# Small TensorE products side by side, packed values in 32-column tiles, one PSUM pool and positions as 512 and 64

## The chip, the cores and the metric

One core of a Trainium2 chip runs the whole kernel. The metric is device time in microseconds (us), the median of several runs. The runs of the two kernels are made on the same chip in the same session. A run more than 1.5% above the fastest run of its kernel is called slow here, and ratios use fast runs alone. TensorE is called PE in the profile, its weight loads PEld; DVE is VectorE, ACT is ScalarE, POOL is GpSimd, SP issues DMA.

## The reference, cut to what matters

```python
# attention: batch 8, heads 8, 576 positions, 64 per head, 32 packed queries
p_packed = sm_attn(p, k, v)                  # 32 rows per head
out = sm_attn(q, p_packed, p_packed)         # 576 rows per head
# gate: x is out as [8, 576, 512]
proj = x @ w_proj                            # x1, x2, x3, 512 columns each
x2_conv = irfft(rfft(x2) * rfft(filter_fft)) # along the 576 positions
y = x1 * x2_conv * x3
return y @ w_out
```

The kernel never forms x. It projects the 32 packed rows of each head (qm), carries the second attention's weights through the Fourier transform, multiplies in the spectrum (f, tt, gm), and comes back with the inverse (x2).

Of the kernel before, what the change touches and what calls it, by code (L numbers as in the profile page):

```python
# [17 lines left out]
P = 128  # L18
# [8 lines left out]

# [4 lines left out]
COL0 = [320, 0, 448, 128, 256]  # L32
HALF = 288
# [4 lines left out]


def _column_t():  # L40
    t = np.zeros(576, dtype=np.int64)
    for i in range(5):
        t[COL0[i]:COL0[i] + TILE_SZ[i]] = TILE_T[i]
    return t


def _constants(S):
# [35 lines left out]
    ac = _f16(inv[:, :, _column_t()].transpose(1, 0, 2))  # L83
# [3 lines left out]
class Op:  # L87


    def __init__(self, n, engine, call, what, args, kw):  # L90
        self.n, self.engine, self.call, self.what, self.args, self.kw = n, engine, call, what, args, kw
        named = dict(kw)
        rest = [a for a in args if isinstance(a, bass.AP)]
        self.out = named.pop("out") if "out" in named else rest.pop(0)
        self.ins = rest + [a for a in named.values() if isinstance(a, bass.AP)]
        self.writes = [r for r in map(region, [self.out]) if r]
        self.reads = [r for r in map(region, self.ins) if r]
        self.columns = max([x.size() // x.shape[0] for x in [self.out] + self.ins[:1]])
        self.need, self.then = 0, []

    def small_tiles(self):
        return self.what == "matmul" and self.ins[0].shape[0] == 64
# [35 lines left out]
class Recorder:  # L138
# [5 lines left out]
    def __init__(self, tc):  # L144
        self.tc, self.ops, self.slot = tc, [], {}
        for name, engine in self.NAMES.items():
            setattr(self, name, self.Engine(self, engine, getattr(tc.nc, name)))

    class Engine:
# [3 lines left out]
        def __getattr__(self, what):  # L153
            def record(*args, **kw):
                ops = self.recorder.ops
                ops.append(Op(len(ops), self.engine, getattr(self.real, what), what, args, kw))
            return record

    def tile(self, pool, shape, dtype, tag, bufs, name):
        t = pool.tile(shape, dtype, tag=tag, name=name, bufs=bufs)  # L160
        self.slot[t.tensor.name] = tag, bufs
        return t

    def depend(self):

        seen, self.users, bank = {}, {}, {}
        for op in self.ops:
            before = set()
            for mine, regions in ((False, op.reads), (True, op.writes)):
                for t, p0, p1, cols in regions:  # L170
                    for o, theirs, q0, q1, c in seen.get(t, ()):
                        if (mine or theirs) and p0 < q1 and q0 < p1 and not cols.isdisjoint(c):
                            before.add(o)
# [13 lines left out]
    def plan(self):  # L187
# [3 lines left out]
        used = dict.fromkeys([tag for tag, _ in self.slot.values()], 0)  # L191
# [4 lines left out]
        window, busy, full, tiling = 3413.0, {}, {0: False}, [False]  # L196
# [16 lines left out]
        def clock(t):  # L213

            for k in range(max(full) + 1, int(t // window) + 1):
                full[k] = busy.get(k - 1, 0) > (0.22 if full[k - 1] else 0.72) * window
            return full[int(t // window)]

        def news(op):
            return {r[0] for r in op.writes + op.reads if r[0] in self.slot and r[0] not in opened}  # L220

        def fits(op):
            more = {}
            for t in news(op):
                tag, bufs = self.slot[t]
                more[tag] = more.get(tag, 0) + 1
                if used[tag] + more[tag] > bufs:
                    return False
# [9 lines left out]
        def issue(e, t):  # L238
            while free[e] <= t + 1e-6:
                op = min((o for o in ready[e] if fits(o)), key=lambda o: o.n, default=None)  # L240
                if op is None:
                    return
                ready[e].remove(op)
                for x in news(op):
                    used[self.slot[x][0]] += 1
                    opened.add(x)
                order.append(op)
                if op.what == "dma_start":
# [3 lines left out]
                    at(t + took + 1500, "start", op)  # L252
                else:
                    if e == "PE":
                        n, fast = op.columns, clock(t)
                        if op.small_tiles():
                            took = 40 if fast else 75
                        else:
                            took = max(n / 2.4 + 2.5, 26) if fast else max(n / 1.2, 45)
                        if op.small_tiles() != tiling[0]:  # L260
                            took += 95
                        tiling[0] = op.small_tiles()
                        k = int(t // window)
                        busy[k] = busy.get(k, 0) + took
                        land = took + (n / 2.4 if op.small_tiles() else 0) + 175
                    else:
                        took = op.ns()
                        land = took + 60
# [5 lines left out]
        for op in self.ops:  # L274
            if op.need == 0:
# [3 lines left out]
        while events:  # L279
            t, _, what, x = heapq.heappop(events)  # L280
            if what == "done":
                release(x, False)
                for r in {r[0] for r in x.reads + x.writes}:
                    if r in left:
                        left[r] -= 1
                        used[self.slot[r][0]] -= left[r] == 0
# [31 lines left out]
def kernel(  # L318
# [31 lines left out]
    ps = ctx.enter_context(tc.tile_pool(name="ps", bufs=3, space=bass.MemoryType.PSUM))  # L350
# [4 lines left out]
    NA = 3  # L355

    def pst(name, shape, dtype=FP32):
        return nc.tile(ps, shape, dtype, "pa", NA, name)

    def psm(name, shape, dtype=FP32):  # L360
        return nc.tile(ps, shape, dtype, "pm", 8 - NA, name)
# [109 lines left out]
    def front(b):  # L471
# [86 lines left out]
        pv = pst(f"pv_b{b}", [P, 2, 4 * D])  # L558
        z1 = pst(f"z1_b{b}", [P, 2])
        for t in range(2):  # L560
            for i in range(KI):
                nc.tensor.matmul(pv[:, t, :], e1[:, i, ts(t, P)], vn[:, 4 * t:4 * t + 4, ts(i, D)],
                                 start=(i == 0), stop=(i == KI - 1))
            for i in range(KI):
                nc.tensor.matmul(z1[:, t:t + 1], e1[:, i, ts(t, P)], ones[0:KP, :],
                                 start=(i == 0), stop=(i == KI - 1))
            if t == 0:
                yield 810
        rz1 = sb([P, 2], FP32, tag="rz1", name=f"rz1_b{b}")
        nc.vector.reciprocal(rz1[:], z1[:])  # L570
        ppn = sb([P, 2, D], FP16, tag="ppn", name=f"ppn_b{b}")
        for u in range(4):
            r = slice(32 * u, 32 * u + 32)
            nc.vector.tensor_tensor(out=ppn[r, :, :], in0=pv[r, :, ts(u, D)],
                                    in1=rz1[r, :].unsqueeze(2).broadcast_to([32, 2, D]), op=ALU.mult)
        yield 810
# [11 lines left out]
        e2 = sb([P, 4, HJ], FP16, tag="e2", name=f"e2_b{b}")  # L588
        e2c = sb([P, P], FP16, tag="e2c", name=f"e2c_b{b}")
        a2n = sb([P, 4, HJ], FP16, tag="a2n", name=f"a2n_b{b}")  # L590
        a2c = sb([P, P], FP16, tag="a2c", name=f"a2c_b{b}")
        zs = sb([P, 5, H], FP32, tag="zs", name=f"zs_b{b}")
        zr = sb([P, 5, H], FP32, tag="zr", name=f"zr_b{b}")

        def normal(sp, e, a, z, r):

            n = z.shape[1]
            nc.scalar.activation(out=e, in_=sp, func=AF.Exp, scale=scale)
            ev = e.rearrange("p (i j) -> p i j", j=NPK)
            nc.vector.tensor_reduce(out=z, in_=ev, axis=AX.X, op=ALU.add)  # L600
            nc.vector.reciprocal(r, z)
            nc.gpsimd.tensor_tensor(out=a.rearrange("p (i j) -> p i j", j=NPK), in0=ev,
                                    in1=r.unsqueeze(2).broadcast_to([P, n, NPK]), op=ALU.mult)

        def score2(ii):
            sp = pst(f"s2_b{b}", [P, 2, HJ])
            for h in range(H):
                x = (h % 2) * 4 + h // 2
                nc.tensor.matmul(sp[:, :, ts(x, NPK)], qT[:, h, ii, :], R[:, x, :], start=True, stop=True)
            i0 = 2 * ii  # L610
            flat = "p i x -> p (i x)"
            normal(sp.rearrange(flat), e2[:, i0:i0 + 2, :].rearrange(flat), a2n[:, i0:i0 + 2, :].rearrange(flat),
                   zs[:, i0:i0 + 2, :].rearrange(flat), zr[:, i0:i0 + 2, :].rearrange(flat))

        def score2_tail():
# [5 lines left out]
            normal(sp[:], e2c[:], a2c[:], zs[:, 4, 0:4], zr[:, 4, 0:4])  # L621

        for ii in range(2):
            score2(ii)
            yield 470
        score2_tail()
        yield 120
        s["a2n"], s["a2c"], s["R"] = a2n, a2c, R

    def turn(b):  # L630
# [5 lines left out]
        def project(c):  # L636
            qp = [pst(f"qp_b{b}", [P, DM]) for u in range(2)]
            for g in range(H // 2):
                for u in range(2):
                    nc.tensor.matmul(  # L640
                        qp[u][g * NPK:(g + 1) * NPK, :], R[u * D:(u + 1) * D, 4 * u + g, (1 - u) * NPK:(2 - u) * NPK],
                        wp[u * D:(u + 1) * D, g, ts(c, DM)], start=True, stop=True)
            for u in range(2):
                nc.scalar.copy(out=qm[:, u, ts(c, DM)], in_=qp[u][:])

        for c in (1, 0, 2):
            project(c)
            yield 460
# [4 lines left out]
        for t in range(2):  # L653
            fp = pst(f"fp_b{b}", [P, DM])
            nc.tensor.matmul(fp[:], a2c[:], wt[:, t, 0:DM], start=True, stop=False)
            for n, i in enumerate((1, 3, 0, 2)):
# [4 lines left out]
            nc.vector.tensor_tensor(out=lohi[:, t, :, 0, :], in0=fp[:, 0:2 * P].rearrange("p (c f) -> p c f", c=2),  # L661
                                    in1=ez[:, t, 1, :, :], op=ALU.add)
            yield 660
        nc.gpsimd.tensor_tensor(out=lohi[:, :, :, 1, :], in0=ez[:, :, 0, :, :], in1=ez[:, :, 1, :, :],
                                op=ALU.subtract)
        fp = pst(f"fpt_b{b}", [P, 2, 64])
        for t in range(2):
            for i in range(4):
                nc.tensor.matmul(fp[:, t, :], a2n[:, i, ts(t, P)], wc[:, i, 256:320], start=(i == 0), stop=False)
            nc.tensor.matmul(fp[:, t, :], a2c[:], wt[:, t, 512:576], start=False, stop=True)  # L670
# [3 lines left out]
        for t in range(2):  # L674
            tp = pst(f"a2tp_b{b}", [P, S], FP16)

            nc.tensor.transpose(tp[:, ds(COL0[4] - 64 * t, P)], a2c[:], ident[:])
            for i in range(4):
                nc.tensor.transpose(tp[:, ds(COL0[i], P)], a2n[:, i, ts(t, P)], ident[:])
# [4 lines left out]
    def middle(b):  # L684
# [4 lines left out]
        w = sb([P, ND, 2, HALF], FP32, tag="w", name=f"w_b{b}")  # L689
# [25 lines left out]
        def gate(m, e):  # L715
# [138 lines left out]
```

## The kernel before: the parts that the change and the argument touch

The kernel is written as four stages per batch (`front`, `turn`, `middle`, `back`). They are recorded as a list of operations. A greedy planner then orders each engine's list with its own idea of durations, and the order it finds is what runs. PSUM's eight banks are divided: three for the attention stages (`pst`), five for the transform (`psm`).

```python
def pst(name, shape, dtype=FP32):
    return nc.tile(ps, shape, dtype, "pa", NA, name)        # NA = 3 banks
def psm(name, shape, dtype=FP32):
    return nc.tile(ps, shape, dtype, "pm", 8 - NA, name)    # 5 banks
...
# packed values: 12 products of 256 columns, a quarter of each is used
pv = pst(f"pv_b{b}", [P, 2, 4 * D])
z1 = pst(f"z1_b{b}", [P, 2])
for t in range(2):
    for i in range(KI):
        nc.tensor.matmul(pv[:, t, :], e1[:, i, ts(t, P)], vn[:, 4 * t:4 * t + 4, ts(i, D)], ...)
    ...                                                     # z1: the sums, by a column of ones
for u in range(4):                                          # ppn: four small normalisations
    r = slice(32 * u, 32 * u + 32)
    nc.vector.tensor_tensor(out=ppn[r, :, :], in0=pv[r, :, ts(u, D)], in1=rz1[r, :]..., op=ALU.mult)
...
# projection of one third: eight small products, 64 x 32 each, into two PSUM tiles
def project(c):
    qp = [pst(f"qp_b{b}", [P, DM]) for u in range(2)]
    for g in range(H // 2):
        for u in range(2):
            nc.tensor.matmul(qp[u][g * NPK:(g + 1) * NPK, :],
                             R[u * D:(u + 1) * D, 4 * u + g, ...], wp[u * D:(u + 1) * D, g, ts(c, DM)], ...)
    for u in range(2):
        nc.scalar.copy(out=qm[:, u, ts(c, DM)], in_=qp[u][:])
...
# sums in the spectrum; first and last batch: two on VectorE, two on GpSimd
even = nc.vector if b in (0, B - 1) else nc.gpsimd
even.tensor_tensor(out=gm[:, 0, :], ...); even.tensor_tensor(out=gm[:, 1, :], ...)
nc.gpsimd.tensor_tensor(out=gm[:, 2, :], ...); nc.gpsimd.tensor_tensor(out=gm[:, 3, :], ...)
...
# inverse: positions as two halves of 288; half e needs gm[2e], gm[2e+1] and gm[4]
def inverse(m, e):
    x2 = psm(f"x2_b{b}", [P, HALF])
    for j in range(3):
        nc.tensor.matmul(x2[:], gm[:, 4 if j == 2 else 2 * e + j, ts(m, P)], ac[:, j, cols], ...)
    nc.vector.scalar_tensor_tensor(out=y[:, m, cols], in0=w[:, m, e, :], scalar=SC_Y, in1=x2[:], ...)
```

The softmax here doesn't subtract the row's maximum and nothing guards it: scores larger than these inputs give would overflow.

## Time and profile before

| | before |
|---|---|
| median | 229.43 us (3 runs, 228.91 to 229.69; 229.17 with the fourth, taken later) |
| span of the profiled run | 226.7 us |
| PE busy | 203.8 us, 90% |
| a steady round (first qTp_b of one batch to that of the next) | 23.88, 22.98, 23.89 us |

Spans are read from the profiled run; here its span is 1.8 us shorter than its device time. A steady round is the time the pipeline takes for one more batch; it is measured between equal instructions and says what the middle of the kernel costs. The lines that carry the reading are in the prediction below.

### The profile page before, as it was taken

What the parts mean: (1) busy time and instruction counts of PE and PEld (TensorE: products, weight loads), DVE (VectorE), ACT (ScalarE), POOL (GpSimd) and SP (SyncE); (2) the same over time, 40 slices, a digit from 0 to 9 for tenths busy, and PEclk for the clock granted to TensorE, in tenths of its full rate; (3) what the DMA queues carried; (4) which work ended last, traced back from release to release, by engine and by line L of the source; (5) the groups of instructions that cost most, each with busy time, mean ns of one, the idle gap of its engine ahead of it and who ended that gap; (6) DMA issues with size and microseconds to landing.
All of it is one profiled execution on the core that took longest, in us unless ns stands there. A gap on an engine that the chain in (4) does not pass through costs nothing.

```text
span 226.7 us, 5282 instructions
## 1 busy us (share of the span) xinstructions
PE 203.8 (90%) x2034; PEld 130.8 (58%) x2034; DVE 167.1 (74%) x388; ACT 138.3 (61%) x301; POOL 134.3 (59%) x120
## 2 busy tenths in 40 slices
PE   0698689997999999899999999999999999989791
PEld 0246446744666686567657766676566756655450
DVE  4428437997639979985898599858987799689850
ACT  2327475564767865875777668865876684624432
POOL 8522285759551898549645894477445944866700
PEclk9999958996999999999999999999999999999999
DMA  5999999999999272959572947112111201311314
GB/s 134 277 233 203 201 201 202 203 193 197 106 180 263 43 107 18 183 84 200 133 119 62 167 158 104 49 48 104 38 49 48 95 0 46 142 48 71 116 69 166
DMA packets 36393, 28.67 MB, mean 126 GB/s; under 512 B 7888, under 2 KB 30928, under 8 KB 36368
## 3 DMA queue, kind: packets, MB, share of 16 engines
q0 software_dynamic: 29312, 16.52, 54.4%
q1 hardware_dynamic: 6336, 11.10, 14.2%
q10 hardware_dynamic: 720, 0.72, 1.0%
q8 instruction: 16, 0.26, 0.5%
q14 instruction: 9, 0.07, 0.1%
HBM read 35.41 MB, written 9.44 MB: 198 GB/s over the span
## 4 chain that ended last, share of the span: by engine, by line
PE 70%; DVE 10%; ACT 7%; POOL 4%; issue 3%; DMA 3%; ACTq 0%; POOLq 0%; DVEq 0%
PE x_b L311 20%; PE o_b L311 12%; PE f_b L311 6%; PE fp_b L311 5%; PE qp_b L311 5%; PE pv_b L311 4%; PE hp L311 4%; PE s_b L311 3%; DMA pn_b<-in_p_dram 3%; PE kTp_b L311 3%; PE qTp_b L311 3%; DVE tt_b L311 2%; POOL tt_b L311 2%; ACT e_b L311 2%; ACT x1s_b L311 2%
## 5 line engine op out<-in xcount | busy, mean ns | idle before, releaser
L311 POOL TENSOR_TENSOR tt_b<-tt_b,tt_b 128x1024 f32<-128x1024 f32 x16 | 37.7, 2358 | 31.0 <-DVE tt_b L311 31.0
L311 PE MATMUL x_b<-a2t_b,qm_b 128*128 128x288 f16 x256 | 43.2, 286 | 0.1
L311 DVE TENSOR_TENSOR tt_b<-f_b,h 128x1024 f32<-128x1024 f32 x32 | 39.0, 1219 | 3.0 <-PE f_b L311 2.8
L311 PE MATMUL x_b<-ac,gm_b 128*128 128x288 f16 x192 | 35.9, 297 | 3.2 <-DVE gm_b L311 1.4
L311 ACT ACTIVATE os_b<-o_b 128x512 f32<-128x512 f32 x36 | 21.5, 598 | 26.5 <-PE o_b L311 26.4
L311 POOL TENSOR_TENSOR gm_b<-tt_b,tt_b 128x512 f16<-128x512 f32 x28 | 36.1, 1319 | 0.6
L311 DVE TENSOR_TENSOR w_b<-x1s_b,x_b 128x288 f32<-128x288 f32 x64 | 28.2, 450 | 7.6 <-ACT x1s_b L311 6.1
L311 PE MATMUL o_b<-wout,y_b 128*128 128x512 f16 x128 | 33.2, 379 | 0.2 <-ACT x1s_b L311 0.2
L311 ACT COPY x1s_b<-x_b 128x288 f32<-128x288 f32 x64 | 25.5, 401 | 12.8 <-PE x_b L311 10.9
L311 ACT CAST qm_b<-qp_b 128x512 f16<-128x512 f32 x48 | 27.3, 595 | 4.8 <-PE qp_b L311 4.6
L311 ACT ACTIVATE e_b<-s_b 96x384 f16<-96x384 f32 (+1 forms) x48 | 24.7, 528 | 6.5 <-PE s_b L311 5.9
L311 DVE SCALAR_TENSOR_TENSOR y_b<-w_b,x_b 128x288 f16<-128x288 f32 x64 | 26.8, 447 | 1.3 <-PE x_b L311 1.2
L311 PEld LDWEIGHTS <-qm_b 128*128 128x128 f16 x256 | 22.5, 97 | 8.3 <-issue 2.7
L311 POOL TENSOR_TENSOR a2n_b<-e_b,zr_b 128x512 f16<-128x512 f16 x16 | 16.4, 1042 | 17.9 <-DVE zr_b L311 6.6
L311 PE MATMUL f_b<-qm_b,fa_b 128*128 128x512 f16 x80 | 25.7, 386 | 0.2 <-ACT os_b L311 0.2
L311 PEld LDWEIGHTS <-gm_b 128*128 128x128 f16 x192 | 17.5, 100 | 14.1 <-issue 5.3
L311 PE MATMUL qp_b<-wp,ppk 64*32 64x512 f16 x192 | 20.5, 398 | 1.7 <-ACT kT L311 0.7
L311 PEld LDWEIGHTS <-a2n_b 128*128 128x128 f16 x192 | 14.6, 102 | 8.0 <-POOL a2n_b L311 1.4
L311 PEld LDWEIGHTS <-y_b 128*128 128x128 f16 x128 | 11.8, 98 | 10.0 <-issue 0.4
L311 PE MATMUL kTp_b<-ident,kn_b 96*128 96x96 f16 x192 | 13.5, 208 | 1.5 <-ACT qm_b L311 1.2
L311 PEld LDWEIGHTS <-e_b 96*128 96x128 f16 x192 | 13.4, 97 | 2.2 <-ACT e_b L311 0.9
L311 PE MATMUL pv_b<-vn_b,e_b 96*128 96x256 f16 x96 | 13.3, 273 | 0.7 <-ACT e_b L311 0.7
(81 smaller groups left out, 334.0 us busy)
## 6 DMA issues: line engine op xcount, KB each, us to landing
out_dram<-os_b SPq DMA_DIRECT2D x32, 256.0 KB, 2.5
kn_b<-in_k_dram POOLq DMA_DIRECT2D x8, 576.0 KB, 10.2
vn_b<-in_v_dram POOLq DMA_DIRECT2D x8, 576.0 KB, 11.3
qn_b<-in_q_dram POOLq DMA_DIRECT2D x8, 512.0 KB, 12.5
wp<-in_moe_w_proj_dram POOLq DMA_DIRECT2D x3, 512.0 KB, 20.3
filt<-in_moe_filter_fft_dram SPq DMA_DIRECT2D x4, 256.0 KB, 6.4
out_dram<-os_b SPq DMA_DIRECT2D x16, 64.0 KB, 1.7
wout<-in_moe_w_out_dram POOLq DMA_DIRECT2D x1, 512.0 KB, 13.3
```

What stands on the lines that cost most here:

```text
L311: ins = op.call(*op.args, **op.kw).ins
```

## The change

Its intent is to take switching and half-used products off TensorE, and fixed costs off the other engines. Small products become units that start together; packed values use 32 columns of the array per head; all eight PSUM banks are one pool with at most six of a kind; positions go as one bank of 512 and a rest of 64 that four blocks share. The planner gets a model of tiles side by side, so every order changes.

```diff
+    def one_unit(self):            # products recorded inside start one after the other
+        self.unit = []
...
-        return nc.tile(ps, shape, dtype, "pa", NA, name)
+        return nc.tile(ps, shape, dtype, "ps", 8, name, ("attention", 6))
-        return nc.tile(ps, shape, dtype, "pm", 8 - NA, name)
+        return nc.tile(ps, shape, dtype, "ps", 8, name, ("transform", 6))
...
-        pv = pst(f"pv_b{b}", [P, 2, 4 * D])
-        z1 = pst(f"z1_b{b}", [P, 2])
+        pv = pst(f"pv_b{b}", [P, 2, D + 1])
+        with nc.one_unit():
+            for t in range(2):
+                for i in range(KI):
+                    for u in range(4):
+                        nc.tensor.matmul(pv[32 * u:32 * u + 32, t, 0:D], e1[:, i, ds((4 * t + u) * NPK, NPK)],
+                                         vn[:, 4 * t + u, ts(i, D)], start=(i == 0), stop=(i == KI - 1))
...  (one ppn for four; one reduce, reciprocal and multiply of 1152 for 512 + 512 + 128, but in batch 0)
-        for c in (1, 0, 2):
-            project(c)
+        for cs in ((1,), (0,), (2,)) if b == 0 else ((1, 0), (2,)):
+            project(*cs)           # inside one_unit: 8 or 16 products
...
+        if b not in (0, B - 1):    # the low halves of fa, on VectorE before
+            nc.gpsimd.tensor_tensor(out=lohi[:, :, :, 0, :], in0=ez[:, :, 0, :, :], in1=ez[:, :, 1, :, :], op=ALU.add)
...
-        def inverse(m, e):
-            x2 = psm(f"x2_b{b}", [P, HALF])
+        def inverse(m):
+            x2 = psm(f"x2_b{b}", [P, MAIN])
+            for e, cols in enumerate((slice(0, EVEN), slice(EVEN, MAIN))):      # 288 and 224 columns
...
+        def inverse_left():        # 64 columns of each of the four blocks, in one bank
+            x2 = psm(f"x2t_b{b}", [P, ND, 64])
...  (gates likewise: four of 512 and one of 4 x 64 for eight of 288; the copy of yt goes)
```

## The prediction

> **What bounds the kernel now.** I read the page first: which engine is busy, and when.
>
> ```profile
> PE 203.8 (90%) x2034; PEld 130.8 (58%) x2034; DVE 167.1 (74%) x388; ACT 138.3 (61%) x301; POOL 134.3 (59%) x120
> PE   0698689997999999899999999999999999989791
> PEclk9999958996999999999999999999999999999999
> DMA  5999999999999272959572947112111201311314
> PE 70%; DVE 10%; ACT 7%; POOL 4%; issue 3%; DMA 3%; ACTq 0%; POOLq 0%; DVEq 0%
> ```
>
> The reader is to see three things. PE is 9 or more in nearly every slice after the sixth, so from about 37 us to about 213 us TensorE sets the pace. Before 37 us DMA is 9 and PE is not: the head waits for loads. In slices 6, 7 and 10 the clock was lower. The chain that ended last agrees: PE is 70% of it.
>
> Second, busy time by stretch. The kernel is a software pipeline with one batch a round; between two equal points of the chain (the first qTp_b) a round takes about 23.6 us. Columns: length, then busy us and count of PE, weight loads, DVE, ACT and POOL.
>
> ```profile
> 97.60:121.50 23.90, 23.54 (x254) 15.74 (x252) 19.25 (x46) 17.06 (x38) 15.54 (x13) 1.00 0.73 128
> 144.50:168.40 23.90, 23.54 (x253) 15.73 (x252) 19.25 (x46) 17.08 (x38) 13.35 (x11) 1.00 0.17 57
> ```
>
> PE has 0.36 us of idle in 23.90; DVE, the next, has 4.65. A busy PE is not yet a useful one, so third I read the chain of waits and the timeline of PE for the spacing of products (start us, length us, what).
>
> ```profile
> 101.85 0.65 PE fp_b L311 x5
> 102.51 0.66 PE pv_b L311 x6
> 103.17 0.13 PE z_b L311 x6
> 104.24 0.86 PE o_b L311 x4
> ...
> 117.70 0.34 PE L311 MATMUL s_b<-pk,kT 128*128 128x64 f16 x6
> 117.97 0.40 PE L311 MATMUL qp_b<-wp,ppk 64*32 64x512 f16 x4
> 118.30 0.54 PE L311 MATMUL x_b<-ac,gm_b 128*128 128x288 f16 x3
> 118.77 0.40 PE L311 MATMUL qp_b<-wp,ppk 64*32 64x512 f16 x4
> 119.10 0.66 PE L311 MATMUL x_b<-a2t_b,qm_b 128*128 128x288 f16 x4
> ...
> 183.83 0.66 PE L311 MATMUL x_b<-a2t_b,qm_b 128*128 128x288 f16 x4
> 184.42 0.41 PE L311 MATMUL qp_b<-wp,ppk 64*32 64x512 f16 x8
> 184.76 0.54 PE L311 MATMUL x_b<-ac,gm_b 128*128 128x288 f16 x3
> ```
>
> Full-array products stand back to back: o_b (512 columns) every 215 ns, pv_b (256) every 110, x_b (288) every 122, z_b (1 column) every 25. Only the small tiles (qp_b, 64*32) break the stream. The last of the six s_b starts at 117.85 and needs 29 ns, so TensorE stands about 94 ns before the group; the next full product starts 329 ns after the group's first. A group of four thus costs 423 ns. At 184.42 eight went side by side for 94 + 342 = 436 ns: twice the work for 3% more time. In this trace the 192 qp_b products went in 46 groups, 42 of them after batch 0, and most were of four or fewer: the order opened one PSUM tile first and its partner later.
>
> **What the Trainium skill says.** "TensorEngine Tiling (Array Packing)", section Tiling Modes, says that changing the tiling mode drains the TensorE and that different tiles load weights and multiply in parallel. The trace agrees: about 94 ns standing on the way in, and on the way out 329 ns against 213 of streaming (512 columns). "TensorE: Matmul & The Clock Gate", section Part 3: Packing small matmuls, gives a span of one product's duration plus about 4 ns for each further tile; the starts of the four at 117.97 are 3 to 5 ns apart, and so are their weight loads. The first page's section Restrictions and Gotchas says that column tiling excludes Fast Weight Load. The trace before does not show whether 32-column loads keep up with short products: every qp_b streams 512 columns. That is my main doubt. "VectorE: DVE Perf Modes", section The TRN2 errata, says that a fixed cost comes once per instruction, so fewer, larger ones pay less. The trace agrees: 447 to 450 ns for 288 columns from PSUM and 686 for 512, that is 1.05 ns a column plus about 147.
>
> **The change part by part, per batch.**
>
> *Projection (qp_b).* Before: 42 groups in batches 1 to 7, six a batch, 6 x 423 = 2.54 us. After: a unit of 16 and a unit of 8. The 8 cost 436 ns. The 16 are two rounds on the same eight tiles, 436 + 213 = 649 ns (estimate from the same rows). Together 1.09 us: 1.45 saved.
>
> *Packed values (pv_b).* Before: 12 products of 256 columns of which a quarter is used, 12 x 110 = 1.32 us. After: 48 products of 64 columns, four side by side, 12 rounds. At the 29 ns that 64-column products take on the full array, a round is about 30 ns: 94 + 12 x 30 + 116 to leave the mode = 0.57 us. Saved 0.75. The z sums stay (12 x 25 ns). If a weight load isn't hidden, a round is 60 ns and the saving 0.4.
>
> *Positions.* Gates: 32 x 122 = 3.90 us before; after, 16 x 215 + 16 x 29 = 3.90. Inverse: 24 x 122 = 2.93; after, 12 x 122 + 12 x 96 + 12 x 29 = 2.96. TensorE gains nothing. DVE and ACT gain fixed costs: w and y 8 x 0.45 each become 4 x 0.686 + 0.416 (-0.43 each); x1s 8 x 0.401 becomes 4 x 0.598 + 0.373 (-0.44 ACT); the copy of yt goes (-0.41 ACT).
>
> *Normalisation.* ppn, four of 287 ns, becomes one (-0.86 DVE). Reduce 2 x 0.657 + 0.228 becomes one of 1152 elements, 1.37 (-0.17); reciprocal 0.68 becomes 0.38 (-0.31). The multiply on POOL, 2 x 1.042 + 0.394, becomes 2.12 (-0.36).
>
> *The low halves of fa.* Two DVE adds of 420 ns go (-0.84) and one POOL add of about 1.27 us comes, in batches 1 to 6.
>
> Sum for a steady round: PE 23.6 - 1.45 - 0.75 = 21.4 us; DVE 19.25 - 3.04 = 16.2; ACT 17.06 - 0.85 = 16.2; POOL 15.5 + 0.9 = 16.4. PE stays the bound with five microseconds in hand, so what PE saves counts in full there, and what the others save counts only where PE waits for them: of the round from 97.6 us some 0.7 us is such waiting (qp_b for a PSUM tile that ACT still reads, s_b for ppk). A common pool of eight banks and fewer openings should save part of it.
>
> *PSUM pool and plan.* Three and five banks become eight, at most six of a kind. A unit starts only when all its tiles are free, so a unit of 16 wants four banks at once.
>
> Over the kernel: batch 0 of both parts lies in the head, which waits for loads and for the chain of ppn; I count 0.5 us for that shorter chain. Batches 1 to 7 lie in the stretch where PE bounds: 7 x (1.45 + 0.75) = 15.4 us. Shorter waits: 1.5. Against it: the end, where the last batch stands alone. The fourth y of 0.68 us must now be done before the first output projection, and only 0.35 us of leftover products cover it: +0.4. And the plan leaves more holes when PE is less loaded; I take 2.0 us back for that. Sum: -0.5 - 15.4 - 1.5 + 0.4 + 2.0 = -15.0, from 229.43 to 214.4 us.
>
> **The rivals.** First, small tiles are slower than I count: weight loads of 32 columns come one after another or can't go under the product on the same tile. Against it: four loads start 3 ns apart at 117.97; for it: no row here has two rounds of short products on one tile. At 27 ns each in a row 48 loads take 1.3 us, as much as today, and the projection's second round starts some 90 ns late: the total saving falls to about 9 us, the time to 220.
>
> Second, a new wait takes the place of the one removed: units starve for four PSUM banks, or a2, which now is one multiply after all exponentials, or fa, whose lower half now comes from POOL, arrives late. For it: the multiply ended at 115.9 us in the round shown, about 3.2 us after the last exponential began; one reduce, reciprocal and multiply take 3.9. Against it: the fp_b that read such a product come at the round's start, after 121 us, so 5 us of slack lie between. If it happened it would be some 0.5 to 1 us a round: 218 to 221.
>
> Third, another engine or the DMA becomes the bound. Sums of 16.4 against 21.4 us speak against it, and DMA is mostly at 1 to 3 after slice 26. In the middle DMA is at 9 in places, but PE waited for a landing only once, 7.9 us at the start. The head stays.
>
> Fourth, the clock: idle PE lets it fall, as in slices 6, 7 and 10 (one window of 6.8 us and one of 3.4). If the order of the early rounds is better, the second goes, about 1.5 us gained; if holes grow, one more comes and costs as much. Also, the whole order is planned afresh, which moves single waits by 1 to 2 us either way.
>
> **Range and chances.** All sure terms (projection 10.1 us, measured on this trace's own groups of eight) already exceed 2%, which is 4.6 us. With rival one or two in full I come to 220 or 221; with the waits gone and no holes to 210. Range 209.5 to 220. Faster by over 2%: 0.95; within 2%: 0.04; slower: 0.01.
>
> **What would show it right or wrong.** PE instructions should rise from 2034 to 2418 (36 more pv_b and 12 more x_b a batch), and DVE's should fall by about 110 to 276. qp_b: 17 units (three in batch 0), not 46 groups, a unit of 8 leaving in about 342 ns and one of 16 in about 555. pv_b: 48 products whose first to the next full product take about 480 ns; 800 or more means that rival one holds. A steady round of 21 to 21.6 us with PE over 95% busy; if PE falls under 90% there, the wait named before fp_b, f_b or qp_b tells which second rival it is. I am wrong altogether if the round stays above 22.8 us, or if the head grows by several microseconds under the new plan.

## The result, and the profile after

The changed kernel took 216.66 us (median of 4, 215.59 to 217.65), against 229.17 us before. The ratio is 0.9453, 95% interval 0.9393 to 0.9513. A ratio here is the mean time of one kernel's fast runs over that of the other's of the same rounds, so it is not quite the ratio of the medians.

The page of the changed kernel: busy times with counts, then PE, granted clock and DMA in 40 slices, then the chain by engine.

```profile
PE 187.0 (87%) x2418; PEld 117.0 (55%) x2418; DVE 149.5 (70%) x276; ACT 127.4 (59%) x269; POOL 140.1 (65%) x112
PE   0777559994999999999999999999999999997890
PEclk9999958997699999999999999999999999999796
PE 65%; DVE 16%; DMA 6%; POOL 5%; issue 3%; ACT 2%; DVEq 0%; POOLq 0%
```

The counts are those foretold, 2418 and 276, and qp_b goes in 16 groups where 17 units were foretold, since two units of the first batch stand together. PE still sets the pace in the middle. But its row has a 4 at about 48 us, and the clock row has low slices there and near the end; this kernel's profiled run had 17 us at half clock before its last product, the kernel before 10.2. (In all 14 traces the clock record knows two values, full and half, and stretches of 3.41 us or a multiple of it, but for a last one that the end of the record cuts. Such a stretch of 3.41 us is called a window below.)

Two of the three steady rounds of the changed kernel (length, then busy and count of PE, weight loads, DVE, ACT, POOL):

```profile
91.34:112.97 21.63, 21.37 (x292) 14.27 (x290) 17.31 (x32) 14.38 (x32) 17.88 (x15) 1.00 0.82 142
133.91:155.30 21.39, 21.25 (x303) 13.76 (x301) 15.74 (x30) 15.28 (x34) 12.62 (x10) 1.00 0.21 63
```

The three rounds took 21.63, 20.94 and 21.39 us, mean 21.3 against 23.6. PE is busy 99% of them. So no other engine took over.

PE's timeline in the changed kernel, a unit of 8, a unit of 16, and the packed values:

```profile
153.60 0.41 PE L344 MATMUL qp_b<-wp,ppk 64*32 64x512 f16 x8
153.95 0.32 PE L344 MATMUL s_b<-pk,kT 128*128 128x64 f16 x5
...
156.97 0.62 PE L344 MATMUL qp_b<-wp,ppk 64*32 64x512 f16 x16
157.53 0.35 PE L344 MATMUL s_b<-pk,kT 128*128 128x64 f16 x6
...
160.91 0.56 PE L344 MATMUL pv_b<-vn_b,e_b 96*32 96x64 f16 x48
161.40 0.39 PE L344 MATMUL f_b<-qm_b,fa_b 128*128 128x512 f16 x1
```

The next full product starts 341 ns after a unit of 8, 557 ns after one of 16 and 489 ns after the first of the 48; foretold were 342, 555 and 480. The starts of the 48 show why: the first four come within 10 ns, the next four start 39 ns after the first, and from there a new four starts every 29 to 30 ns. The loads of 32 columns hide under products of 64, so the first rival fell without an experiment.

**Where the time went.** I took every start of a PE product in both traces and split the step to the next start into the product's own streaming, what half clock adds to it, the switching of the tiling mode, and the rest, which is waiting. This runs from the first product to the start of the last.

| from 35 us on, us | before | after | change | foretold |
|---|---|---|---|---|
| full products | 152.8 | 143.2 | -9.6 | |
| small products and mode switches | 17.7 | 11.2 | -6.5 | |
| both: PE's work | | | **-16.1** | -15.4 |
| waiting | 13.7 | 14.5 | +0.8 | -1.5 + 2.0 |
| half clock | 1.9 | 4.2 | **+2.3** | 0 |
| start of the kernel, to 35 us | | | -0.3 | -0.5 |
| last product's start to the end | 5.2 | 6.0 | +0.8 | +0.4 (the whole end) |
| sum (spans 226.7 and 214.1) | | | -12.6 | -15.0 |

The work went as foretold. The missing 2.4 us are for the most part the clock. The last 0.8 us is a transfer: the last write of the end goes in other pieces. These are the page's lines of the writes (count, KB each, us to landing), before and then after:

```profile
out_dram<-os_b SPq DMA_DIRECT2D x16, 64.0 KB, 1.7
```

```profile
out_dram<-os_b SPq DMA_DIRECT2D x16, 128.0 KB, 2.4
```

Before, the last output tile went as four writes of 64 KB; now as two of 128 KB, which take 0.7 us longer to land, and nothing follows to hide it. The later traces agree: from the last product's start to the end it is 5.2 to 5.3 us in every kernel with the positions as before and 6.0 us in every one with the new positions.

The end of the changed kernel, where the last batch stands alone (timeline of all engines; a bracket is idle time before, and who ended it):

```profile
197.46 2.37 DVE L344 TENSOR_TENSOR gm_b<-tt_b,tt_b 128x512 f16<-128x512 f32 x2
197.50 3.45 POOL L344 TENSOR_TENSOR gm_b<-tt_b,tt_b 128x512 f16<-128x512 f32 x2
198.21 0.66 PE L344 MATMUL x_b<-ac,gm_b 128*128 128x288 f16 x4 [1.30 <-DVE gm_b L344]
199.34 0.20 PE L344 MATMUL x2t_b<-ac,gm_b 128*128 128x64 f16 x1 [0.47 <-POOL gm_b L344]
199.88 0.51 PE L344 MATMUL x_b<-ac,gm_b 128*128 128x288 f16 x3 [0.35 <-DVE gm_b L344]
```

PE stands three times, 2.1 us in all, for the four sums of gm. In the clock record the window from 200.7 to 204.1 us is then at half speed, and every inverse in it takes twice its time. The same happens for the first batch: PE stands 2.0 and 1.0 us before 50.4 and 52.1 us, and the clock is at half from 50.5 to 57.3.

### The profile page after: what moved, and what is told of

Same layout as the page of the kernel before. It is cut to its first block, busy times and chain, and to the rows that moved or that the text cites. A ratio compares the mean times of both kernels' runs of the same rounds, so it can differ in the third digit from the quotient of the medians.

```text
span 214.1 us, 5815 instructions
## 1 busy us (share of the span) xinstructions
PE 187.0 (87%) x2418; PEld 117.0 (55%) x2418; DVE 149.5 (70%) x276; ACT 127.4 (59%) x269; POOL 140.1 (65%) x112
## 4 chain that ended last, share of the span: by engine, by line
PE 65%; DVE 16%; DMA 6%; POOL 5%; issue 3%; ACT 2%; DVEq 0%; POOLq 0%
PE x_b L344 20%; PE o_b L344 13%; PE f_b L344 7%; DMA kn_b<-in_k_dram 6%; PE fp_b L344 6%; PE s_b L344 4%; DVE tt_b L344 3%; PE qTp_b L344 3%; DVE gm_b L344 3%; PE pv_b L344 2%; DVE zs_b L344 2%; PE kTp_b L344 2%; PE qp_b L344 2%; POOL gm_b L344 2%; PE a2tp_b L344 2%
## 5 line engine op out<-in xcount | busy, mean ns | idle before, releaser
L344 PE MATMUL x_b<-a2t_b,qm_b 128*128 128x512 f16 (+1 forms) x256 | 42.0, 286 | 0.4 <-DVE w_b L344 0.3
L344 PE MATMUL x_b<-ac,gm_b 128*128 128x288 f16 (+1 forms) x192 | 30.5, 295 | 5.0 <-DVE gm_b L344 4.7
L344 PEld LDWEIGHTS <-gm_b 128*128 128x128 f16 x288 | 22.9, 104 | 15.0 <-DVE gm_b L344 5.7
L344 POOL TENSOR_TENSOR fa_b<-ez_b 128x512 f16<-128x512 f32 x14 | 17.5, 1269 | 14.7 <-ACT ez_b L344 14.7
L344 ACT COPY x1s_b<-x_b 128x512 f32<-128x512 f32 (+1 forms) x40 | 22.3, 560 | 8.2 <-PE x_b L344 8.0
L344 DVE TENSOR_TENSOR w_b<-x1s_b,x_b 128x512 f32<-128x512 f32 (+1 forms) x40 | 24.9, 625 | 1.6 <-ACT x1s_b L344 1.4
L344 PEld LDWEIGHTS <-a_b 128*128 128x128 f16 x240 | 17.1, 101 | 11.6 <-POOL a_b L344 2.8
L344 DVE SCALAR_TENSOR_TENSOR y_b<-w_b,x_b 128x512 f16<-128x512 f32 x32 | 20.3, 678 | 3.2 <-PE x_b L344 3.1
L344 POOL TENSOR_TENSOR a_b<-e_b,zr_b 128x1152 f16<-128x1152 f16 (+2 forms) x10 | 17.3, 1742 | 0.7 <-DVE zr_b L344 0.5
L344 ACT COPY ez_b<-fp_b 128x512 f32<-128x512 f32 x16 | 9.8, 610 | 12.2 <-PE fp_b L344 12.2
L344 PEld LDWEIGHTS <-kn_b 96*128 96x128 f16 x192 | 10.5, 97 | 3.9 <-DMA kn_b<-in_k_dram 1.3
```

Source lines behind the costliest of these rows:

```text
L344: ins = op.call(*op.args, **op.kw).ins
```

## The experiments

Each ran beside the kernel before on the same chip. The theory after the first look: the prediction's sum is right, part by part. Its rivals: that another part of the change than the one named did the work, and that the end's loss is the waits and not the clock. Each edit makes the planner order the whole kernel anew from the point that it touches, which has to be kept in mind. The sessions used different chips, so kernels of different runs are compared by their ratios to the kernel before.

### One part undone at a time

**Packed values as before.** The 12 products, z1 and four ppn put back into the changed kernel.

```diff
-        pv = pst(f"pv_b{b}", [P, 2, D + 1])          # and its unit of 48
+        pv = pst(f"pv_b{b}", [P, 2, 4 * D])          # and z1, ppn as before
```

> The changed kernel with the packed values as they were (12 products of 256 columns, sums in a tile of their own, four ppn). Theory of the sum: the packed form is worth 0.75 us in each of seven rounds, so 216.7 + 5.3 = 222 us and a steady round of 22.1 us against 21.3. Rival, that the gain is mostly the units and the common pool and the 48 short products give little: within 1.5 us of the changed kernel, 216.7 to 218.

Measured: 222.64 us, ratio to before 0.9694 (0.9622 to 0.9767). Against the 0.9453 of the changed kernel the packed values are worth 2.4%, 5.5 us (by the two intervals, 1% more or less). The steady rounds were 22.6, 22.1 and 21.9 us. The theory held, the rival fell.

**No units.**

```diff
-            with nc.one_unit():
+            if True:
-        for cs in ((1,), (0,), (2,)) if b == 0 else ((1, 0), (2,)):
+        for cs in ((1,), (0,), (2,)):
```

> The changed kernel with the projection recorded third by third and no unit, so that the plan may split it; the common pool stays. Theory of the sum: groups of four come back, six a batch, 1.45 us a round, 226 to 227 us. Rival, that the pool of eight banks is what lets eight products start side by side: the groups become of eight by themselves (three a batch, 1.31 us against 1.09), and the time is 217.5 to 219.5.

Measured: 219.23 us, ratio 0.9563 (0.9471 to 0.9655). This is the rival's number. The timeline of PE shows how:

```profile
147.20 0.41 PE L344 MATMUL qp_b<-wp,ppk 64*32 64x512 f16 x8
147.54 0.43 PE L344 MATMUL kTp_b<-ident,kn_b 96*128 96x96 f16 x6
```

From batch 4 on every third of the projection went as eight by itself. The steady rounds averaged 21.2 us, no longer than with units. So the unit is worth about 1.1%, with intervals that reach from nothing to about 2%, and none of it shows in the rounds.

**Positions as before.**

```diff
-COL0 = {1: 0, 3: 128, 4: 256, 0: 384}
-EVEN, MAIN = 288, 512
+COL0 = [320, 0, 448, 128, 256]
+HALF = 288               # gate(m, e), inverse(m, e), project_out, yt as before
-        return nc.tile(ps, shape, dtype, "ps", 8, name, ("transform", 6))
+        return nc.tile(ps, shape, dtype, "ps", 8, name, ("transform", 5))
```

> The changed kernel with the positions as before: two halves of 288, eight gates, eight inverses, the copy of yt. (With six banks for the transform the plan stops short, so it has five there.) Theory of the sum: TensorE's time is the same, so a steady round stays within 0.2 us of 21.3; DVE and ACT have some 0.9 us more each, which costs nothing. The end, where even columns can go first, should be up to 2 us shorter: 214.5 to 217 us. Rival, that the fewer and larger evacuations matter for the round: the round grows by 0.5 us or more and the time to 220 or more.

Measured: 210.61 us, ratio 0.9168 (0.91 to 0.9236). It is faster by 3% than the changed kernel, and faster than either theory had it. My count of this trace from 35 us on gives the same PE work within 0.5 us, 15.2 us of waiting against 14.5, and 0.1 us of half clock against 4.2. The clock row of its page shows no dip after the start:

```profile
PEclk9999856999999999999999999999999999999999
```

So in this build the new positions bring a loss, about 4 us of it through the clock and 0.8 us through the last write. The expected steady round was missed: 25.7, 21.8 and 22.5 us.

```profile
84.09:109.79 25.70, 25.40 (x327) 16.48 (x325) 20.83 (x44) 20.30 (x45) 20.18 (x15) 1.00 0.83 143
109.79:131.64 21.85, 20.97 (x287) 14.23 (x285) 16.70 (x37) 14.38 (x34) 16.77 (x13) 1.00 0.72 127
131.64:154.16 22.52, 22.12 (x291) 14.89 (x288) 17.77 (x37) 17.79 (x41) 14.18 (x9) 1.00 0.17 60
```

The first of them is no steady round: 327 products of PE lie in it against 287 and 291, because the first stage had run ahead and the others caught up. The other two stream as many columns as the second and third round of the changed kernel (57,484 and 59,532), and are 0.9 and 1.1 us longer (20.94 and 21.39 us there). So the rival was right about the round, and wrong about the time. The starts of the first output product of batches 0, 2, 4 and 6 show both sides: with the positions as before they come 7.0, 6.0, 4.0 and 2.6 us earlier than in the changed kernel, and the end comes 4.7 us earlier. In these two traces the new positions lose some 7 us up to the first output product, win back 4.4 us over the next six batches, and lose 2 us at the end. Whether the fewer evacuations or the sixth bank of the transform shorten the rounds is not shown, since this run changed both.

**None of the three.**

```diff
+  (the three edits above together, the transform again with six banks)
```

> Neither units, nor packed values, nor the new positions: what is left of the change is the common pool, the new plan, one normalisation and the low halves of fa on GpSimd. Theory of the sum: these relieve engines that don't bound, so 226 to 229 us, a steady round of 23.2 to 23.6. Rival, that the pool removes most of the switching: 221 to 224 us, a round near 22.5, with qp_b in groups of eight.

Measured: two fast runs, 219.72 and 220.52 us, and two slow ones, 226.49 and 226.89 at a mean clock of 0.939. The ratio of the fast runs is 0.9581 (0.9478 to 0.9684). The projections of the steady rounds went mostly in groups of eight, the rounds took 22.9, 22.6 and 22.9 us. The rival was right about the groups; the time is a little under its range and the round a little over its 22.5. What is left of the change still saves 4%, by two fast runs.

**Also with the old PSUM pools.**

```diff
-        return nc.tile(ps, shape, dtype, "ps", 8, name, ("attention", 6))
+        return nc.tile(ps, shape, dtype, "pa", 3, name, ("attention", 3))
-        return nc.tile(ps, shape, dtype, "ps", 8, name, ("transform", 6))
+        return nc.tile(ps, shape, dtype, "pm", 5, name, ("transform", 5))
```

> As the run with neither units, packed values nor positions, but with the PSUM banks divided again, three and five. What is left of the change is the plan's constants, the one normalisation and fa on GpSimd. Theory that the common pool is what put eight projections side by side: the groups of four come back (six a batch), a round of 23.3 to 23.6 us, 227 to 230 us. Rival, that the plan or the lighter other engines did it: stays at 222 to 224.5 us.

Measured: 226.90 us, ratio 0.9895 (0.9847 to 0.9942), a hair under the expected range; steady rounds of 23.4, 23.6 and 23.3 us. The groups of four are back, as PE's timeline shows:

```profile
157.84 0.40 PE L350 MATMUL qp_b<-wp,ppk 64*32 64x512 f16 x4
158.17 0.30 PE L350 MATMUL x_b<-a2t_b,qm_b 128*128 128x288 f16 x1
158.40 0.40 PE L350 MATMUL qp_b<-wp,ppk 64*32 64x512 f16 x4
```

From 0.9895 to 0.9581 is 3.1%, 7.2 us: that is the common pool alone, by the two intervals 1.1% more or less. The three steady rounds show 0.6 us each of it; the rest arose outside them. The lighter normalisation, fa on GpSimd and the plan's constants together are the remaining 1%.

**Units with the old pools.** If side by side is all that counts, a unit should do alone what the pool did alone.

```diff
   (positions as before and packed values new, from the run of 210.6 us; units of eight)
-        return nc.tile(ps, shape, dtype, "ps", 8, name, ("attention", 6))
+        return nc.tile(ps, shape, dtype, "pa", 3, name, ("attention", 3))     # transform: "pm", 5
```

> Units of eight and the packed values, positions as before, but the PSUM banks divided again, three and five. Theory that side by side is what counts, by whatever means: the unit does alone what the common pool did alone, three units of eight a batch cost 1.31 us against 1.09, so 212 to 213.5 us against 210.6. Rival, that the common pool brings more than that (fewer waits for a bank): 215 us or more, with the waits before PE's products longer in the steady rounds.

Measured: fast runs of 214.39, 216.46 and 216.48 us and three slow ones; ratio 0.9385 (0.9317 to 0.9453). Every projection after the first batch went in eights. The time is nearer the rival's, but its mechanism is not there: the three steady rounds sum to 70.1 us in both traces. In the profiled run the difference arose before 90 us, with 6.8 us of half clock from 50.8 us on. That run was one of the slow ones (217.76 us), so where the 2.2% of the fast runs arose is not shown. So in the rounds, a unit of eight without the pool does as well as with it; the pool's further gain lies outside them.

### The clock or the waits

**Useless products in the standstills.** Six products of 512 columns, whose result nobody reads, behind the last gate of the first and last batch. The output stays correct.

```diff
         gate(*range(ND))
+        if b in (0, B - 1):
+            keep = psm(f"keep_b{b}", [P, DM])
+            for r in range(6):
+                nc.tensor.matmul(keep[:], fa[:, 0, 0:P], qm[:, 0, ts(1, DM)], start=True, stop=True)
```

> The changed kernel plus twelve useless products of 512 columns, six behind the last gate of the first batch and six behind that of the last, where TensorE stood still for 2 to 3 us waiting for gm. Theory of the clock: the new positions cost their 6 us because these standstills let the granted clock fall to half for the windows that follow; the extra products keep it up, the half-speed windows after 45 us go, and the time falls by 2 to 4 us, to 213 to 215, although 1.3 us of work is added twice. Rival, that the waits themselves are the cost: no gain, 216.5 to 219 us.

Measured: 214.54 us, ratio 0.9347 (0.9305 to 0.9390), 1.1% below the changed kernel, with 2.6 us of work added. At the end it is as clean as such a test can be:

```profile
196.83 1.24 PE L344 MATMUL keep_b<-qm_b,fa_b 128*128 128x512 f16 x5
198.08 0.66 PE L344 MATMUL x_b<-ac,gm_b 128*128 128x288 f16 x4
199.20 0.20 PE L344 MATMUL x2t_b<-ac,gm_b 128*128 128x64 f16 x1 [0.46 <-POOL gm_b L344]
199.75 0.42 PE L344 MATMUL x_b<-ac,gm_b 128*128 128x288 f16 x2 [0.34 <-DVE gm_b L344]
```

The inverses start when they did (43.1 us after the last batch's first qTp_b in both traces), with the same waits of 0.46 and 0.34 us. But there is no half-speed window, and the last output product starts 51.47 us after that point, not 52.96. The clock alone cost 1.5 us there. At the first batch it did not work: the plan put the six products ahead of a projection, PE still stood 1.7 and 1.3 us behind it, and one window at half clock (52.7 to 56.1 us) came all the same, where the changed kernel had two. So the theory holds at the end; at the first batch this run does not test it.

**The sums of gm on one engine.** "GPSIMD Engine Reference", section Architecture, says that GpSimd has one physical read port and one write port to SBUF and shares both with VectorE. In the changed kernel both engines do sums of gm at once.

```diff
-                nc.gpsimd.tensor_tensor(out=gm[:, 2, :], ...)      # and gm[:, 3, :]
+                even.tensor_tensor(out=gm[:, 2, :], ...)           # VectorE in the first and last batch
```

> The changed kernel with all four gm sums of the first and last batch on VectorE, none on GpSimd. In the trace of the changed kernel two sums on VectorE took 2.4 and 4.0 us beside GpSimd's, where 0.7 us each would be expected alone. Theory that the two engines slow each other: four sums take about 2.8 us, TensorE's wait at the end falls from 2.1 to about 1.2 us, and with the clock windows the time is 213 to 215.5. Rival, that VectorE is then simply the longer queue: 216 to 218 us.

Measured: 210.78 us, ratio 0.9176 (0.9131 to 0.9220): the theory's direction, and more than it gave. The planned order is the same in the steady rounds, which took 21.63, 20.94 and 21.39 us, exactly as in the changed kernel, so the gain lies outside them: of the 6.6 us between the two spans, 1.4 stood before the first sum of gm, 2.6 more came before the steady rounds and 2.5 after them. At the end the four sums took 2.50 us in a row where two had taken 2.37. The traces show more than a slowing. In the changed kernel's end the first sum took 0.69 us; the second began 0.57 us after GpSimd's first and took 1.76, until 0.55 us after that one's end. In the 14 traces, all 33 VectorE sums of gm that began during a GpSimd sum or multiply ended 0.55 us after it. So VectorE seems to stand until GpSimd's instruction is done. It need not be a sum: in this run the first sum of the first batch still took 2.36 us, behind GpSimd's multiply for a2.

**The last batch alone.**

```diff
+                odd = nc.vector if b == B - 1 else nc.gpsimd
```

> The changed kernel with the four gm sums of the last batch alone on VectorE; the plan before the end is the same. It separates the end from the first batch. Theory that the end cost 2.5 us of the 2.9 us missing from the prediction (sums on two engines, 2.1 us of standstill, then a window at half clock): 213.5 to 215 us. Rival, that the gain of the earlier run came from the first batch and from chance: 216 to 217.5 us.

Measured: 213.56 us, ratio 0.9286 (0.9239 to 0.9334), 1.8% under the changed kernel; the theory held. Its end, to set against that of the changed kernel:

```profile
196.69 2.50 DVE L344 TENSOR_TENSOR gm_b<-tt_b,tt_b 128x512 f16<-128x512 f32 x4
197.44 2.23 PE L344 MATMUL x_b<-ac,gm_b 128*128 128x288 f16 x17 [1.31 <-DVE gm_b L344]
```

One wait of 1.31 us is left, the other two are gone, and no window at half clock follows. From the last batch's first qTp_b to the end it is 56.5 us against 59.0. The other part of the earlier run's gain, 0.9286 to 0.9176, is by difference the first batch.

**The same edits where the positions are as before.** First in both ends, then in the last batch alone.

> The run with the positions as before (210.6 us, the fastest so far), with the gm sums of the first and last batch on VectorE alone. If the two engines slow each other, the wait of 1.1 us at the end is cut to about 0.3 and the time falls to 208.5 to 210; if not, it stays at 210.5 or rises.

Measured: 215.06 us, ratio 0.9352 (0.9302 to 0.9403): a clear miss. Here the edit cost 4.5 us against 210.6. Its trace shows why no mechanism is to be read from it: the plan around the first batch came out otherwise, PE stands 2.0 and 1.5 us before 50.8 and 53.0 us, and the clock is at half from 51.8 to 58.6. Its first qTp_b starts 1.9 us later too (23.2 against 21.3 us), long before any sum of gm.

> The run with the positions as before (210.6 us), with the four gm sums of the last batch alone on VectorE, so that the order of the first batches, which the earlier try upset, stays as it was. Expected: the wait of 1.1 us at the end falls to about 0.4 us: 209.3 to 210.3 us, the fastest of all. If 210.6 or more, the wait at the end is not set by the sums.

Measured: 210.71 us, ratio 0.9157 (0.9109 to 0.9205), the same as without the edit (0.9168) within its interval. PE's wait before the inverses is gone, but a wait of 0.4 us for y comes behind them, and from the last batch's first qTp_b the end is only 0.2 us shorter. This wait was not what set that end.

**Useless products in the first standstill, with all sums on VectorE.**

```diff
+        if b in (0,):            # six products as above, in the run of 210.8 us
```

> All gm sums of the first and last batch on VectorE (210.8 us), plus six useless products of 512 columns behind the first batch's last gate, where 2.0 us of standstill and a window at half clock remained at 49 us. If the clock is what costs, the half-speed window after 45 us goes and 0.5 to 1.5 us are gained: 209.3 to 210.3. If the wait itself is the cost: 210.8 to 212.

Measured: 211.88 us (median of six, two of them slow), ratio of the fast runs 0.9191 (0.9134 to 0.9247), no gain. It does not decide: the planner put the six products ahead of a projection, PE still stood 1.7 us before 51.6 us, and the half-speed window (52.0 to 55.4 us) came all the same.

No kernel gave a wrong result. Three are about level as the fastest: positions as before (0.9168), that with the last sums on VectorE (0.9157), and the changed kernel with all sums of both ends on VectorE (0.9176). Each beats both given kernels, by about 8% and 3%.

## Why the prediction was right or wrong

*The bound.* Right. PE set the pace before and after; a round fell from 23.6 to 21.3 us where 21.4 was foretold, and PE was 99% busy in it. DVE, ACT and POOL had 16.7, 14.8 and 16.0 us a round where 16.2, 16.2 and 16.4 were foretold.

*Packed values.* Right: 5.3 us foretold, 5.5 measured by undoing them. The doubt, rival one, is settled by the 29 ns between rounds of short products.

*Projection.* The size was right and the author of it wrong. The step that reads "After: a unit of 16 and a unit of 8 ... 1.45 saved" credits the unit. I had written myself that groups of four arose because one PSUM tile was opened first and its partner later, and then gave the gain to the unit and only "part of" 0.7 us of waiting to the pool. The pool alone made groups of eight (7.2 us); the unit on top of it brought about 2.5 us, not clear of the noise and none of it in the rounds.

*Positions.* "TensorE gains nothing" was right for its work. What the sum left out is that they set the order of the ends. With 288-column halves all four even halves can go before the odd sums are there; with banks of 512 and a shared rest the plan put a product of the rest in front, which waited for GpSimd. Undone, the kernel is 3% faster. That this is a loss of the positions themselves is not shown: with gm on one engine the kernel with new positions is as fast. The loss belongs to positions, split sums and plan together. The sum also left out a gain: the steady rounds are about 1 us shorter with the new positions and the sixth bank, at equal work, where the prediction had 1.5 us of shorter waits for the whole kernel.

*The end.* This is the term that was mis-sized. "+0.4" for the end, and the clock a mere rival at 1.5 us either way, became +0.8 for the last write and, with the first batch, +2.3 for the clock; 1.5 of that was measured at the end. I had looked for the wait for y and had not asked what the wait for gm, 1.4 us in the profile before, would set off. Half clock, the fourth rival, was the one that came true in full ("one more comes and costs as much"), twice.

*Holes.* The 2.0 us taken back for them were not seen in the rounds; together with shorter waits I had +0.5 and it was +0.8.

*Range.* 216.66 us lies in 209.5 to 220.0, and 2.3 us above the central value. Two errors of attribution inside, the pool and the positions, did not show in it. In part that is luck: what the positions won in the rounds, 4.4 us, took back about half of what they lost before and after them.

## What to carry to other kernels

When small products go in smaller groups than they could, look first for the buffer that their partners lack; a bigger pool can do what a scheduling rule is written for. A standstill of TensorE costs its own length and can cost a second time, through the clock of the window behind it: here 2.1 us of standing drew 1.5 us more, one wait of 1.31 us drew nothing. Shorten it, or keep the array streaming through it, and check in the trace that the planner put the products where you meant them. A sum that comes out right does not prove its terms, so undo the parts one by one, and read a whole-order scheduler's single results with a few us of luck in mind.

## What the Trainium skill lacked or had wrong

- "TensorE: Matmul & The Clock Gate", Part 1: The HAM clock gate, gives one idle window of about 3.4 us as what returns the clock to half. In the 14 traces a window need not be idle. I counted the columns streamed in each 3.41 us window, small tiles by their share of the array. All 27 windows at full clock that were followed by half clock before the kernel's last product had 3104 columns or fewer, about 38% of the 8,100 that fit (from the 215 ns of 512 columns); all 716 that kept the clock had 2948 or more.
- "TensorEngine Tiling (Array Packing)", Restrictions and Gotchas, lists Fast Weight Load as lost with column tiling and gives no cost. None showed: 96x32 loads hid under products of 64 columns, 29 ns from one round of four to the next.
- The same page, Tiling Modes, names the drain without a size. Here it was 92 to 95 ns into the small tiles, and the next full product started about 106 ns after their streaming ended.
- "GPSIMD Engine Reference", Architecture, says that the port is shared with VectorE and gives no figure for what that costs. A VectorE sum of two 512-column fp32 operands took 0.63 to 0.69 us with GpSimd free; begun during a GpSimd sum or multiply it took 1.1 to 2.4 us and ended 0.55 us after that instruction, in all 33 cases.
